# Inverse transform in pairs of 64-row tiles, spectra stored channel by channel, and a rewritten order

## The chip, the cores and the metric

One core of a Trainium2 chip runs the whole program. The time is that of one execution on the device in microseconds (us). The core has TensorE (PE; its weight loads are listed apart as PEld), VectorE (DVE), ScalarE (ACT), GpSimd (POOL) and SyncE (SP), and 16 DMA engines. Here all DMAs are issued by SP, in one queue.

## The reference

Two independent branches over 2048 positions and 576 channels in bfloat16, put side by side in the output.

```python
# A: a 4-tap causal filter over positions, times v; a long causal convolution by FFT; times q
k_shift = sum(k_pad[:, t:t + S, :] * shift_k[:, ks - 1 - t] for t in range(ks))
kv = k_shift * v
y_f = rfft(kv padded to 2S) * rfft(ssm_k padded to 2S)
y = irfft(y_f)[:S] + kv * ssm_D
a = q * y
# B: linear attention, 32 heads of 18 channels; phi(t) = (t + 1 if t > 0 else exp(t)) + 1e-6
pq, pk = phi(q), phi(k)                       # q, k, v = x @ wqkv
kv, z = einsum(pk, v), einsum(pk)             # sums over all positions
o = einsum(pq, kv) / (einsum(pq, z) + 1e-6)
b = o @ wo
```

## The kernel before

A kernel object (`Prog`) first collects about 800 operations with what each reads and writes. Then `PLAN`, a string written out by a planner beforehand, gives the order of all of them and the engine of each (`P` PE, `D` DVE, `A` ACT, `G` POOL, `S` SP), and `PLACES` gives the memory place of each buffer. An engine runs its own in this order. Products of two tensors ("two" operations) on DVE and POOL are made to follow one another.

Branch A. Position 16a + b lies on partition a, row b. The short filter (`conv_piece`, six pieces: three of 192 channels by two halves of b) is done by DVE with two products (`tap`, L374), one sum of 3072 columns, one of 1536, and a product with v (`tap+` and `tapv`, L229, by DVE or POOL); its second half needs the second load of k (`kh1`). The long convolution is an FFT in two steps. The filter `ssm_k` is loaded in six pieces of 96 channels (`hs`), transposed on PE (`htr`, L404) and evicted into `hT` (`hev`). `s1` multiplies by table G (L427, eight groups of four matmuls for each of three channel chunks; `s1h` for the filter, `s1u` for the signal, evicted to `Ch` and `Cu`). `s2` handles nine pieces of 64 channels: DVE transposes 32x32 blocks (`ct`, L447), PE does the 16-point step in 32-row array tiles (L457, four groups of four), and ACT or DVE evict the spectrum (`sph`, `spu`). `inv` exchanges real and imaginary rows by two DMAs (`X`) and makes the two products `p1` and `p2` (L229). The inverse 16-point step has two forms. For five pieces (`i1`, L515) a strided view of the products is the weight and a 128x128 block-diagonal table moves, so the result lands transposed in `V`:

```python
nc.tensor.matmul(o[:, 128 * c8:128 * c8 + 128],
                 lhsT=view(src.t[:], 4 * hh + c8, [[16, 128]]),
                 rhs=Esb.t[:, 32 + wi, :], start=(wi == 0), stop=(wi == 1))
```

For the four pieces in `TM` (`i1t`, L494) the table is the weight in 32-row tiles, the result is evicted to `yt`, and DVE transposes it into `V` (`tri`, L504). `inv2` does the last step with table E (L541, `i2`), for three groups of 192 channels; the result is evicted (`yb`, `yev`) and multiplied by q (`yq`), or multiplied by q straight from PSUM (`i2q`), and stored.

Branch B. x is loaded in four tiles and transposed (`xtr`, L315 and L313). `kproj` (L580) gives phi(k) through an exponential on ACT (L585) and one DVE instruction (`kphi`, L588); `qproj` (L601) does the same into `pqT` (ACT L604, DVE `qphi` L607). `b_G` (L630) sums x by pk over all positions; `kv` (L664), `den` (L700), a reciprocal and the folded output weight `M` (L720, L744) follow. The reciprocal goes through DRAM (`rw`, `rr`) to be spread, and five DVE products (`pqn`, L229) divide `pqT`. Each of the 32 groups of the output projection (`b_out`, L759, five matmuls) reads all five chunks of `pqT` and all of `M`; its result is evicted to `ob` (`oev`) and stored.

The helpers `copy` (L222 on ACT, L224 on DVE), `tt` (L229) and `dma` (L215) carry the evictions, products and DMAs of all steps, so those lines mix many groups.

Of the kernel before, what the change touches and what calls it, by code (L numbers as in the profile page):

```python
# [13 lines left out]
S = 2048  # L14
# [9 lines left out]
TM = [5, 6, 7, 8]  # L24
# [155 lines left out]
def kernel(  # L180
# [18 lines left out]
    G_d = nc.inline_tensor(Gt.reshape(128, -1), name="tab_g").ap()  # L199
# [75 lines left out]
    for i in range(2):  # L275
        load("Gsb", Gsb, lambda e, i=i: dma(e, Gsb.t[:, 8 * i:8 * i + 8].rearrange("p a b c -> p (a b c)"), G_d[:, 2048 * i:2048 * i + 2048]),
             524288, 4096, wr=[(Gsb, i)])
# [18 lines left out]

    def xt_load(g):
        load("x", x_sb, lambda e: dma(e, x_sb.t[:, 4 * g:4 * g + 4, :].rearrange("p a d -> p (a d)"),
                                      ap(x, 4 * g * D, [[16 * D, 128], [1, 4 * D]])),
# [4 lines left out]
        xTg.append(b)  # L304
        for t0, tn in ((0, 2), (2, 2), (4, 1)):
# [85 lines left out]
    hT = [SB("hT%d" % c, [128, 16, CC]) for c in range(3)]  # L391

    def h_piece(i):
        cc, hh = i // 2, i % 2
        hs = SB("hs", [96, S])
        load("hs", hs, lambda e: dma(e, hs.t[:], A_ssm_k[96 * i:96 * i + 96, :]), 393216, 4096, engs=EARLY)
        for half in range(2):
            ps = psb(1, "hps")

            def tr(e, half=half, ps=ps):  # L400
                o = ps.t.rearrange("p b c -> p (b c)").bitcast(BF)
                hv = hs.t[:].rearrange("d (a b) -> d b a", b=16)
                for j in range(8):
                    nc.tensor.transpose(out=o[:, 128 * j:128 * j + 96], in_=hv[:, 8 * half + j, :],  # L404
                                        identity=ident()[0:96, 0:96])

            def ev(e, half=half, ps=ps):
                i_ = ps.t.rearrange("p b c -> p (b c)").bitcast(BF).rearrange("p (j c) -> p j c", c=128)[:, :, 0:96]
                copy(e, hT[cc].t[:, 8 * half:8 * half + 8, 96 * hh:96 * hh + 96], i_)
            P.op("P", tr, rd=[hs, idw], wr=[ps], name="htr", mm=[(96, 96, 128)] * 8, st="htr%d" % i)  # L410
            P.op("DA", ev, rd=[ps], wr=[(hT[cc], (hh, half))], name="hev", n=768, x2=1, st="htr%d" % i)
        P.op("DG", lambda e: tt(e, hT[cc].t[0:1, 0, 96 * hh:96 * hh + 96], hT[cc].t[0:1, 0, 96 * hh:96 * hh + 96],
                                Drow.t[0:1, 96 * i:96 * i + 96], ALU.add),
             rd=[Drow], wr=[(hT[cc], (hh, 0))], name="hD", n=96, two=1, st="htr%d" % i)

    def s1(cc, nm):
        C = SB("C" + nm, [128, CC // 2, 32, 2])
        for ri in range(2):
            for bg in range(4):
                ps = psb(2, "s1ps")  # L420

                def mm(e, ri=ri, bg=bg, ps=ps):
                    for j in range(4):
                        b = 4 * bg + j
                        src = hT[cc].t[:, b, :] if nm == "h" else vs[bg // 2].t[:, b % 8, CC * cc:CC * cc + CC]
# [8 lines left out]
                rdk = [(vs[bg // 2], cc)] if nm == "u" else [hT[cc]]  # L434
# [7 lines left out]
    def s2(C, cc, pp, nm):  # L442
# [8 lines left out]
        sp = SB("sp" + nm, [128, 4, 512])  # L451
        for kh in range(4):
            ps = psb(1, "s2ps")

            def mm(e, kh=kh, ps=ps):
                for j in range(4):
                    nc.tensor.matmul(  # L457
                        ps.t[32 * j:32 * j + 32, 0, :].rearrange("p (k w t) -> p w k t", w=8, t=2),
# [3 lines left out]
            P.op("AD", lambda e, kh=kh, ps=ps: copy(e, sp.t[:, kh, :], ps.t[:, 0, :]),  # L462
# [10 lines left out]
    def inv(g, su):  # L473
# [5 lines left out]
        xb = SB("X", [128, 4, 512])  # L479
# [6 lines left out]
        if g in TM:  # L486
            yt = SB("yt", [128, 4, 512])
            for j in range(4):
                ps = psb(1, "i1ps")

                def mmt(e, j=j, ps=ps):
                    for kh in range(4):
                        for wi, src in ((0, tx), (1, xb)):
                            nc.tensor.matmul(  # L494
                                ps.t[32 * kh:32 * kh + 32, 0, :].rearrange("p (w k t) -> p k w t", w=8, t=2),
                                lhsT=Esb.t[32 * j:32 * j + 32, 32 + wi, 32 * j:32 * j + 32],
                                rhs=src.t[32 * j:32 * j + 32, kh, :], start=(wi == 0), stop=(wi == 1))
# [10 lines left out]
        for hh in range(4):  # L508
            ps = psb(1, "i1ps")

            def mm(e, hh=hh, ps=ps):
                o = ps.t.rearrange("p b c -> p (b c)")
                for c8 in range(4):
                    for wi, src in ((0, tx), (1, xb)):
                        nc.tensor.matmul(o[:, 128 * c8:128 * c8 + 128],  # L515
                                         lhsT=view(src.t[:], 4 * hh + c8, [[16, 128]]),
                                         rhs=Esb.t[:, 32 + wi, :], start=(wi == 0), stop=(wi == 1))
            P.op("P", mm, rd=[tx, xb, Esb], wr=[ps], name="i1", st=st, mm=[(128, 128, 128)] * 8)
# [4 lines left out]
            P.op("AD", ev, rd=[ps], wr=[(V[gi], (g, hh))], name="i1ev", n=512, st=st)  # L523
# [47 lines left out]
    def kproj(r):  # L571
# [5 lines left out]
        def mm(e):  # L577
            for hh in range(2):
                for t in range(5):
                    nc.tensor.matmul(ps.t[:, hh, 0:HALF],  # L580
                                     lhsT=xT.t[0:KT[t], t, 128 * (r % 4):128 * (r % 4) + 128],
# [169 lines left out]
    def b_out(r):  # L751
        ob = SB("ob", [128, D])
        for hh in range(2):
            ps = psb(1, "ops")

            def mm(e, hh=hh, ps=ps):
                for c, (h0, hn) in enumerate(HCH):
                    kn = 128 if c == 4 else hn
                    nc.tensor.matmul(ps.t[:, 0, 0:HALF], lhsT=pqT.t[0:kn, c, 128 * r:128 * r + 128],  # L759
# [5 lines left out]
        load("oo", None, lambda e: dma(e, ap(outd, 2 * D * r + D, [[32 * D, 128], [1, D]]), ob.t[:]), 147456, 1152, rd=[ob], wr=[])  # L765
# [4 lines left out]
    for cc in range(3):  # L770
        h_piece(2 * cc)
        h_piece(2 * cc + 1)
# [34 lines left out]
S27 S9 S7 P29 G0 A6 G2 P31 G3 S19 G4 G1 G55 P23 A28 D30 S12 D20 S352 P25 P21 A32 G14 S52 S51 P353 D22 S346 P355 A24  # L807
A26 P15 A16 D354 G357 D356 P33 P99 P93 S11 P347 S35 A100 D101 S57 P349 A94 D34 D348 G5 G351 D350 P96 G36 P370 D95
# [81 lines left out]
```

## Time and profile before

| | |
|---|---|
| runs (us) | 173.22, 173.25, 175.86; median 173.25 |
| the profiled execution: time, span | 173.95, 172.2 |
| busy us: PE, PEld, DVE, ACT, POOL | 159.2, 117.8, 144.8, 135.0, 66.2 |
| mean granted TensorE clock | 0.996 |
| DMA packets, MB, mean GB/s | 16327, 30.08, 175 |
| HBM read, written (MB) | 20.12, 4.98 |
| PE matmuls of the steps that change: L515, L494, L457, L404 | 160, 128, 288, 96 |

The span runs from the first to the last instruction of one execution; the time adds what lies around it. Busy time of an engine is the union of its instructions. A group in the profile reads: line, engine, operation, output <- inputs, shapes, count, then busy us and mean ns of one, then idle time just before it and what ended it. Instructions on one engine overlap a little, so count times mean can exceed the busy time.

### The profile page before, as it was taken

The page shows a single profiled execution, that of the slowest core. Times are in us where ns is not written, and L with a number is a line of the kernel's source. Part 1 is how long each engine was busy: PE and PEld are TensorE (multiplying, and loading weights), DVE is VectorE, ACT ScalarE, POOL GpSimd, SP SyncE. Part 2 cuts the span into 40 slices and gives each one's busy share as a digit, 9 for nine tenths or more (in the row PEclk, how much of TensorE's full clock was granted, in tenths as well). Part 3 has the DMA queues.
Part 4 walks back from the last instruction along what each step waited for, and adds up shares of the span by engine and source line. Part 5 has one row for each costly group of instructions (what it writes and reads, how often), then busy time and mean ns, then how long its engine had stood idle before and what let it go on. Part 6 is the DMA issues. An engine that isn't in the chain of part 4 may idle for free.

```text
span 172.2 us, 4216 instructions
## 1 busy us (share of the span) xinstructions
PE 159.2 (92%) x1718; PEld 117.8 (68%) x1718; DVE 144.8 (84%) x169; ACT 135.0 (78%) x239; POOL 66.2 (38%) x38
## 2 busy tenths in 40 slices
PE   0499999989999999999999999999999999998991
PEld 0386887736657766667666788759679766676880
DVE  0140799997999999999999999989979999989871
ACT  3334497969999999999999988899699999875200
POOL 7013100154009994291193001889560900473000
PEclk9999999999999999999999999999999999999998
DMA  5999999993000097800034339945148992176795
GB/s 161 267 235 322 245 287 238 271 265 86 7 2 0 0 292 244 313 11 0 0 126 166 130 67 308 296 149 197 61 131 272 253 354 124 41 214 174 233 272 175
DMA packets 16327, 30.08 MB, mean 175 GB/s; under 512 B 7571, under 2 KB 12308, under 8 KB 15540
## 3 DMA queue, kind: packets, MB, share of 16 engines
q1 hardware_dynamic: 16308, 29.82, 58.5%
q8 instruction: 13, 0.21, 0.5%
q14 instruction: 6, 0.05, 0.1%
HBM read 20.12 MB, written 4.98 MB: 146 GB/s over the span
## 4 chain that ended last, share of the span: by engine, by line
PE 44%; DMA 25%; DVE 19%; issue 6%; ACT 3%; SPq 1%; ACTq 0%; DVEq 0%
PE ps_all L630 12%; DMA wq<-in_B_wqkv_dram 10%; DMA kh<-in_A_k_dram 10%; PE ps_all L515 6%; DVE pqT L607 5%; PE ps_all L427 5%; PE ps_all L759 5%; DVE m L374 4%; PE ps_all L601 4%; DMA x_sb<-in_B_x_dram 4%; PE ps_all L457 4%; PE ps_all L541 3%; DVE pqT L229 2%; DVE m L229 2%; PE ps_all L664 1%
## 5 line engine op out<-in xcount | busy, mean ns | idle before, releaser
L601 PE MATMUL ps_all<-xT,wq 128*126 128x512 bf16 (+3 forms) x100 | 24.1, 381 | 0.4 <-DMA wq<-in_B_wqkv_dram 0.3
L580 PE MATMUL ps_all<-wk,xT 128*128 128x288 bf16 (+1 forms) x160 | 23.4, 299 | 0.3 <-DVE pk L588 0.3
L229 POOL TENSOR_TENSOR m<-m 128x1536 bf16<-128x1536 bf16 x5 | 15.5, 3103 | 16.8 <-ACT GT L641 7.2
L374 DVE TENSOR_TENSOR m<-kh,Wj 128x3072 bf16<-128x3072 bf16 x12 | 20.6, 1748 | 0.4 <-DMA kh<-in_A_k_dram 0.4
L759 PE MATMUL ps_all<-M,pqT 126*128 126x288 bf16 (+1 forms) x160 | 20.7, 285 | 0.2 <-DVE pqT L229 0.2
L222 ACT ACTIVATE Cu<-ps_all 128x768 bf16<-128x768 f32 x23 | 18.5, 865 | 1.6 <-PE ps_all L630 1.1
L580 PEld LDWEIGHTS <-xT 128*128 128x128 bf16 (+1 forms) x160 | 16.0, 102 | 5.3 <-issue 0.9
L222 ACT ACTIVATE sph<-ps_all 128x512 bf16<-128x512 f32 x33 | 19.0, 612 | 0.2 <-PE ps_all L457 0.2
L229 POOL TENSOR_TENSOR sph<-spu,sph 128x2048 bf16<-128x2048 bf16 x3 | 12.3, 4093 | 17.2 <-DVE X L229 15.2
L427 PEld LDWEIGHTS <-Gsb 128*128 128x128 bf16 x192 | 16.4, 98 | 3.6 <-issue 0.8
L759 PEld LDWEIGHTS <-pqT 126*128 126x128 bf16 (+1 forms) x160 | 15.3, 97 | 4.8 <-DVE pqT L229 0.5
L222 ACT ACTIVATE spu<-ps_all 128x512 bf16<-128x512 f32 x29 | 16.3, 609 | 2.0 <-PE ps_all L457 1.7
L601 PEld LDWEIGHTS <-wq 128*126 128x126 bf16 (+3 forms) x100 | 12.4, 131 | 7.7 <-issue 0.9
L222 ACT ACTIVATE ob<-ps_all 128x288 bf16<-128x288 f32 x21 | 7.9, 413 | 12.1 <-PE ps_all L759 11.5
L630 PE MATMUL ps_all<-pk,x_sb 128*128 128x288 bf16 (+1 forms) x128 | 17.1, 287 | 0.0
L222 ACT ACTIVATE Ch<-ps_all 128x768 bf16<-128x768 f32 x21 | 16.9, 848 | 0.2 <-PE ps_all L427 0.2
L588 DVE SCALAR_TENSOR_TENSOR pk<-ek,ps_all 128x576 bf16<-128x576 bf16 x16 | 11.8, 739 | 5.5 <-ACT ek L585 5.5
L585 ACT ACTIVATE ek<-ps_all,neg 128x576 bf16<-128x576 f32 x16 | 12.0, 750 | 4.8 <-PE ps_all L580 3.1
L229 POOL TENSOR_TENSOR hT<-hT,Drow 1x96 bf16<-1x96 bf16 x5 | 3.7, 746 | 30.2 <-DVE hT L224 12.9
L630 PEld LDWEIGHTS <-x_sb 128*128 128x128 bf16 x128 | 12.1, 97 | 4.2 <-issue 1.3
L604 ACT ACTIVATE eq<-ps_all,neg 126x512 bf16<-126x512 f32 (+1 forms) x20 | 13.4, 712 | 0.5 <-PE ps_all L601 0.3
L457 PE MATMUL ps_all<-ct,idw 32*32 32x512 bf16 x288 | 13.8, 382 | 0.0
(97 smaller groups left out, 347.8 us busy)
## 6 DMA issues: line engine op xcount, KB each, us to landing
X<-sph SPq DMA_DIRECT2D x18, 256.0 KB, 2.8
x_sb<-in_B_x_dram SPq DMA_DIRECT2D x4, 576.0 KB, 3.9
hs<-in_A_ssm_k_dram SPq DMA_DIRECT2D x6, 384.0 KB, 10.3
v<-in_A_v_dram SPq DMA_DIRECT2D x2, 1152.0 KB
q<-in_A_q_dram SPq DMA_DIRECT2D x1, 2304.0 KB
out_dram<-ob SPq DMA_DIRECT2D x16, 144.0 KB, 2.0
out_dram<-q SPq DMA_DIRECT2D x12, 192.0 KB, 2.5
rb<-r_scr SPq DMA_DIRECT2D x4, 504.0 KB
```

The lines of the kernel that those rows point to most:

```text
L222: nc.scalar.activation(out=o, in_=i, func=ACTF.Copy)
L229: return (nc.vector if e == "DVE" else nc.gpsimd).tensor_tensor(out=o, in0=a, in1=b, op=op)
L374: return nc.vector.tensor_tensor(out=m.t[:, i:i + 2], in0=i0, in1=i1, op=ALU.mult)
L427: nc.tensor.matmul(ps.t[:, bank, lo - 384 * bank:hi - 384 * bank], lhsT=Gsb.t[:, b, ri, :], rhs=src[:, lo - CC * j:hi - CC * j], start=Tru ...
L457: nc.tensor.matmul(ps.t[32 * j:32 * j + 32, 0, :].rearrange("p (k w t) -> p w k t", w=8, t=2), lhsT=W2()[32 * kh:32 * kh + 32, :], rhs=ct. ...
L580: nc.tensor.matmul(ps.t[:, hh, 0:HALF], lhsT=xT.t[0:KT[t], t, 128 * (r % 4):128 * (r % 4) + 128], rhs=wk.t[0:KT[t], t, HALF * hh:HALF * hh ...
L585: P.op("A", lambda e: nc.scalar.activation(out=eb.t[:], in_=ps.t[:, :, 0:HALF], func=ACTF.Exp, bias=neg1.t[:]), rd=[ps, neg1], wr=[eb], na ...
L588: P.op("D", lambda e: nc.vector.scalar_tensor_tensor(out=pk.t[:, r, 0:D].rearrange("p (h c) -> p h c", h=2), in0=eb.t[:], scalar=1.0, in1= ...
L601: nc.tensor.matmul(ps.t[0:hn, 0, :], lhsT=wq.t[0:KT[t], t, h0:h0 + hn], rhs=xT.t[0:KT[t], t, :], start=(t == 0), stop=(t == 4))
L604: P.op("A", lambda e: nc.scalar.activation(out=eb.t[0:hn], in_=ps.t[0:hn, 0, :], func=ACTF.Exp, bias=neg1.t[0:hn, :]), rd=[ps, neg1], wr=[eb],
L630: nc.tensor.matmul(ps.t[0:m, 0, 0:n], lhsT=x4.t[:, r, 0:65] if t == 4 else x_sb.t[:, r, 128 * t:128 * t + 128], rhs=pk.t[:, r, HALF * hh:H ...
L759: nc.tensor.matmul(ps.t[:, 0, 0:HALF], lhsT=pqT.t[0:kn, c, 128 * r:128 * r + 128], rhs=M.t[0:kn, c, HALF * hh:HALF * hh + HALF], start=(c ...
```

## The change

1. `s2` writes its PSUM bank with the channel outermost, and the spectra `sph`, `spu` and `X` become [128, 16, 128] (channel, then position index) where they were [128, 4, 512].
2. `TM` becomes empty: all nine pieces take the form `i1`. A piece is done in two halves into two PSUM banks. Each 128-row matmul becomes two of 64 rows, one for each half of the array's rows (z), with the 64 columns of its own block of the table, each into its own bank, with a column step of eight. One eviction of 1024 columns follows each half.
3. The filter comes in pieces of 128 channels (four of 128, one of 64) into one `hT` of 576 channels.
4. The table G lies in DRAM with rows of 2304 values, of which 2048 are read.
5. A tile of x holds 512 consecutive positions, four on each partition; the stores of branch B follow that order. A second way to load x (`XD`) is written but its list is empty.
6. `PLAN` and `PLACES` are new: 774 operations for 820. On PE all eight `s1h` groups of the first chunk stand ahead of the first `kproj`; on SP three tiles of x, two filter pieces and both halves of G stand ahead of most of wk; the 32 output groups stand at the very end.

```diff
-TM = [5, 6, 7, 8]
+TM = []
+XD = []
...
-    G_d = nc.inline_tensor(Gt.reshape(128, -1), name="tab_g").ap()
+    Gp = np.zeros((2, 128, 2304), Gt.dtype)
+    Gp[:, :, 0:2048] = Gt.reshape(128, 2, 2048).transpose(1, 0, 2)
+    G_d = nc.inline_tensor(Gp.reshape(256, 2304), name="tab_g").ap()
...
+    def cols(t, r):
+        if r // 4 in XD:
+            return view(t, r % 4, [[4, 128]])
+        return t[:, 128 * (r % 4):128 * (r % 4) + 128]
...
-                                      ap(x, 4 * g * D, [[16 * D, 128], [1, 4 * D]])),
+                                      ap(x, 512 * g * D, [[4 * D, 128], [1, 4 * D]])),
...
-    hT = [SB("hT%d" % c, [128, 16, CC]) for c in range(3)]
+    hT = SB("hT", [128, 16, D])
     def h_piece(i):
-        cc, hh = i // 2, i % 2
-        hs = SB("hs", [96, S])
+        h0, hn = 128 * i, min(128, D - 128 * i)
+        hs = SB("hs", [hn, S])
...
-        sp = SB("sp" + nm, [128, 4, 512])
+        sp = SB("sp" + nm, [128, 16, 128])
...
-                        ps.t[32 * j:32 * j + 32, 0, :].rearrange("p (k w t) -> p w k t", w=8, t=2),
+                        ps.t[32 * j:32 * j + 32, 0, :].rearrange("p (w t k) -> p w k t", w=8, t=2),
                         lhsT=W2()[32 * kh:32 * kh + 32, :], rhs=ct.t[32 * kh:32 * kh + 32, 8 * j:8 * j + 8],
...
-            P.op("AD", lambda e, kh=kh, ps=ps: copy(e, sp.t[:, kh, :], ps.t[:, 0, :]),
+            P.op("AD", lambda e, kh=kh, ps=ps: copy(
+                e, sp.t[:, :, 32 * kh:32 * kh + 32], ps.t[:, 0, :].rearrange("p (c k) -> p c k", c=16)),
...
-        for hh in range(4):
-            ps = psb(1, "i1ps")
+        for hh in range(2):
+            ps = psb(2, "i1ps")
             def mm(e, hh=hh, ps=ps):
-                for c8 in range(4):
+                for c in range(8):
                     for wi, src in ((0, tx), (1, xb)):
-                        nc.tensor.matmul(o[:, 128 * c8:128 * c8 + 128],
-                                         lhsT=view(src.t[:], 4 * hh + c8, [[16, 128]]),
-                                         rhs=Esb.t[:, 32 + wi, :], start=(wi == 0), stop=(wi == 1))
+                        for z in range(2):
+                            nc.tensor.matmul(view(ps.t, 512 * z + c, [[8, 64]]),
+                                             lhsT=src.t[64 * z:64 * z + 64, 8 * hh + c, :],
+                                             rhs=Esb.t[64 * z:64 * z + 64, 32 + wi, 64 * z:64 * z + 64],
+                                             start=(wi == 0), stop=(wi == 1))
...
-                copy(e, view(V[gi].t[:], c0 + 4 * hh, [[n, 32], [16, 4], [1, 4]]),
-                     ps.t.rearrange("p b c -> p (b c)").rearrange("p (c j r) -> p r j c", j=4, r=32))
+                copy(e, view(V[gi].t[:], c0 + 8 * hh, [[16, 4], [n, 32], [1, 8]]),
+                     ps.t.rearrange("p b (j r c) -> p (b j) r c", r=32, c=8))
...
-        load("oo", None, lambda e: dma(e, ap(outd, 2 * D * r + D, [[32 * D, 128], [1, D]]), ob.t[:]), 147456, 1152, rd=[ob], wr=[])
+        load("oo", None, lambda e: dma(e, ap(outd, 2 * D * (512 * (r // 4) + r % 4) + D, [[8 * D, 128], [1, D]]), ob.t[:]), 147456, 1152, rd=[ob], wr=[])
...
-        h_piece(2 * cc)
-        h_piece(2 * cc + 1)
+        for i in ((0, 1), (2,), (3, 4))[cc]:
+            h_piece(i)
```

More of the change, by code (lines that the diff above doesn't have):

```diff
@@ L403, in tr @@
                 for j in range(8):
[L404 to L405 removed]
+                    nc.tensor.transpose(out=o[:, 128 * j:128 * j + hn], in_=hv[:, 8 * half + j, :],
+                                        identity=ident()[0:hn, 0:hn])
             def ev(e, half=half, ps=ps):
[L408 to L414, printed above, removed]
+                i_ = ps.t.rearrange("p b c -> p (b c)").bitcast(BF).rearrange("p (j c) -> p j c", c=128)[:, :, 0:hn]
+                copy(e, hT.t[:, 8 * half:8 * half + 8, h0:h0 + hn], i_)
+            P.op("P", tr, rd=[hs, idw], wr=[ps], name="htr", mm=[(hn, hn, 128)] * 8, st="htr%d" % i)
+            P.op("DA", ev, rd=[ps], wr=[(hT, (i, half))], name="hev", n=8 * hn, x2=1, st="htr%d" % i)
+        P.op("DG", lambda e: tt(e, hT.t[0:1, 0, h0:h0 + hn], hT.t[0:1, 0, h0:h0 + hn], Drow.t[0:1, h0:h0 + hn], ALU.add),
+             rd=[Drow], wr=[(hT, (i, 0))], name="hD", n=hn, two=1, st="htr%d" % i)
     def s1(cc, nm):
```

98 lines of the change are left out of this document (51 added, 47 removed), and 29 rows, old and new, of the table PLACES.

## The prediction

> **What bounds the kernel now.** I read the busy shares first, then the engines by stage, then who waits in the long stage, then the single rows around the change.
>
> ```profile
> PE 159.2 (92%) x1718; PEld 117.8 (68%) x1718; DVE 144.8 (84%) x169; ACT 135.0 (78%) x239; POOL 66.2 (38%) x38
> ```
>
> PE looks like the bound. The busy time by stretches, cut at the start of the first short-filter product on DVE (31.06) and at the end of the last division product (143.62), corrects that. The columns are start:end, length, then busy time and instructions of each engine, granted clock, DMA share and GB/s.
>
> ```profile
> 0.00:31.06 31.06, 23.98 (x238) 19.84 (x239) 14.98 (x24) 16.51 (x23) 6.57 (x16) 1.00 0.97 254
> 31.06:143.62 112.56, 110.98 (x1230) 79.24 (x1227) 108.36 (x116) 105.23 (x186) 53.10 (x18) 1.00 0.49 154
> 143.62:172.20 28.58, 24.26 (x253) 18.73 (x253) 21.43 (x32) 13.29 (x33) 6.54 (x4) 0.97 0.58 169
> ```
>
> In the middle 112.56 us PE is busy 110.98, DVE 108.36 and ACT 105.23: three engines are full at once, so taking work from one alone gains nothing there. The first stretch is a load stage (DMA share 0.97), the last is the output projection. The waits of DVE inside the middle stretch, the longest first, are tiny:
>
> ```profile
> DVE M L224 <- POOL sph L229: 0.9, 1, 0.9
> DVE pqT L607 <- ACT eq L604: 0.5, 1, 0.5
> ```
>
> Two rows of DVE's order in time mark the hinges: the first filter product, and the division products (pqn), without which no output projection can start, because every one reads all five chunks of pqT.
>
> ```profile
> 31.06 1.74 DVE L374 TENSOR_TENSOR m<-kh,Wj 128x3072 bf16<-128x3072 bf16 x1
> ...
> 138.99 4.63 DVE L229 TENSOR_TENSOR pqT<-pqT,rb 126x2048 bf16<-126x2048 bf16 x4
> ```
>
> So the span of 172.2 is 31.06 (to the first product) + 112.5 (DVE's row up to the last pqn) + 28.6 (what is left). I forecast each of the three.
>
> The rows of the changed steps, groups with shapes kept apart:
>
> ```profile
> L457 PE MATMUL ps_all<-ct,idw 32*32 32x512 bf16 x288 | 13.8, 382 | 0.0
> L515 PE MATMUL ps_all<-Esb,sph 128*128 128x128 bf16 x80 | 11.4, 228 | 0.3 <-ACT spu L222 0.3
> L515 PE MATMUL ps_all<-Esb,X 128*128 128x128 bf16 x80 | 11.3, 227 | 0.0
> L494 PE MATMUL ps_all<-sph,Esb 32*32 32x512 bf16 x64 | 3.5, 381 | 0.1
> L504 DVE STREAM_TRANSPOSE V<-yt 128x1024 f32<-128x1024 f32 x4 | 7.7, 1957 | 0.8 <-ACT yt L222 0.8
> L222 ACT ACTIVATE V<-ps_all 128x512 bf16<-128x512 f32 x15 | 8.5, 624 | 0.0
> ```
>
> Instructions overlap their neighbours, so I price by the distance between starts when an engine runs back to back: on DVE the row's mean less 0.08 us (four pqn in 4.63: 1.14 each, mean 1.217), on ACT the mean less 0.13 (512 columns: 0.48, not 0.61). On PE eight L515 matmuls start 62 ns apart, 128x128 transposes 56, 512 columns 216.
>
> **The change, part by part.** *Inverse 16-point step on PE.* Before: five pieces of 32 matmuls (20 groups, 10.9 us from start to next start) and four pieces in 32-row tiles (16 groups, 4.3 us). After: nine pieces of 64 matmuls of 64 rows by 64 columns, in 18 halves of 32, each alternating between two row tiles and two banks. No row shows such a tile. Lower end: both row tiles run at once, 16 rounds of 64 columns; 512 take 216 ns and 128 take 56, so 64 take 29, a half 0.47. Upper end: each weight load follows the other at L515's 62 ns, a half 2.0. The nearest row is L457: 24 of its small tiles, with 24 loads, take 0.62 us (110.66 on), 26 ns a pair against 216 for one alone, so row tiles and their loads do run together. I take 0.5: 9.0 us, and 1.9 for the eight places at which PE enters this tile size (a 64-row matmul among 128-row ones stretches two intervals from 58 to 150 and 195 ns in L664: 0.23). The 32-row runs fall from 29 to 21 without the four pieces: 17.1 us to some 10.3 (0.33 alone, 0.68 for six). Together PE's inverse and 16-point steps go from 28.1 to 21.2.
>
> [...]
>
> *The same step elsewhere.* DVE loses four transposes (1.83 to 1.88 each, 7.4) and seven evictions (0.59, 4.1). ACT has 18 evictions of 1024 columns for 29 of 512: 1024 is 0.92 (between 0.48 for 512 and 1.03 for Wj's 1152), so 16.5 for 13.9: +2.6.
>
> *Spectra channel by channel.* Same matmuls, copies and X transfers, other strides. Matmul writes now go 32 words apart where pairs were adjacent; ends: 0, or half speed, 0.22 more in some 30 rounds, 6.5 us on PE. L457 already writes with gaps at full speed: 0.
>
> *Filter pieces of 128.* 96 transposes become 80 at 62 ns: PE -1.0. Six loads become five with the same bytes; twelve evictions of 768 become ten, eight of them of 1024: DVE gets seven of 0.61 for five of 0.48 (+1.8), ACT three for seven (-2.9).
>
> *Padded table rows, x in blocks of four consecutive rows.* Bytes and instructions stay. 1.05 MB at 245 GB/s is 4.3 us, at the best slice's 322 it is 3.3: a gain of 0 to 1.0 ahead of the forward step; none shows for x or for the output rows, which follow x. I take 0, behind loads that are queued anyway.
>
> *New plan.* This decides. **First stretch:** SP now queues three x tiles, two filter pieces and both halves of the table G before most of wk; G's end is 3.98 MB down the queue (4.70 before). At the slices' 161 to 322 GB/s 4.0 MB are in by 16.5, and x0 landed 2.4 later than this count says (8.67 in the chain): 19. PE then does all eight s1h groups (L427) before any k projection. Transposes do not bring it to full speed (16 took 1.87 us at 4.86 and 1.07 at 33.73; the first 20 of L580 took 4.21, later 20 2.63), so these eight take 4 us, not 2.6. Six k groups of 1.24, one htr and one s1h follow: 31.5; exp and min/max of k4 (0.65 each) stand ahead of the first product: 32.4, against 31.06. kh, now 7.0 MB down the queue instead of 6.7, lands by 30 and is no bound.
>
> **Middle:** DVE's row from the first product to the last pqn. Out: six i1 evictions 3.5, one V transpose 1.8, one ct transpose now earlier 1.2, two GT 0.9, one v product 0.9, one spectrum eviction 0.6, gcol 0.2. In: four products p1, p2 (L229, 1.14 each) 4.6, four yb evictions 1.9, xT 1.2, s1 0.9, a tap sum 0.9, filter 0.8, M 0.7, i2q 0.5, hD 0.1. That is 107.1 before, 109.5 after; DVE's gaps were 5.4 and I keep them. kh's second half waits on another buffer now (kh0, free after the sixth product) and lands 6.9 later with 6.3 of DVE work ahead of it, a wait of 0.6 where 0.4 was. On SP the load of q (2.4 MB) now stands ahead of the reciprocal's way out and back: free after G at some 112, 10 us at 245 GB/s, done before the reciprocal is (125); the way back (3.6 and another 10) is in by 139, ahead of the first pqn at 141. POOL's products fall from 66 to 64 us and stay beside DVE's. The last pqn ends at 32.4 + 109.5 + 5.4 = 147.3, 3.7 later than before. ACT agrees: 101.4 of work from there to the last V eviction (100.0 before in the same 112.4) ends at 145.4, and the plan puts one i2 product, which needs V, ahead of the last pqn. From k4's end PE has 107 left (21.2 as above, 85.7 of other groups at their distances), ends them by 139 and waits some 8 us: that is where its saving goes, and it is the cover for the upper ends above.
>
> **Last stretch:** before, PE had eight i1t, eight i2 groups and 32 projection groups left and DVE 20.7 us. After, 32 x 0.617 + 2 x 0.33 = 20.4 on PE against 12.2 on DVE; the last matmul's end lay 3.8 before the span's. 24.2, against 28.6.
>
> **Sum:** 147.3 + 24.2 = 171.5, 0.7 below 172.2. The profiled execution took 173.95, inside the 173.22 to 175.86 of the runs shown but 0.7 above their median; on the median of 173.25 the sum gives **172.5**.
>
> **Rivals.** *The saving shows whole.* DVE's total falls by 4.4 (142.1 to 137.7 by these prices), ACT's by 3.9, PE's by 7. If the kernel is paced by totals, not by this order, 173.25 - 4.4 = 168.9. For it: three full engines all lose work. Against: DVE's saving lies behind the last pqn, where PE sets the end. Chance 0.20.
>
> [...] Chance 0.08.
>
> *The forward step ahead of k starves DVE.* If G lands as late as 22.5, the first product goes to 36 and the end to 176.1; slower than now from 33.1 on. For it: 19 rests on one lag, and nothing else feeds DVE then. Against: 2 MB of slack in front of kh. Chance 0.17 for over 1 us slower, about half of it over 2%.
>
> *The new strides halve PSUM writes.* 6.5 on PE, under the cover of 8: 172.5 to 174, inside the forecast's range. Chance 0.05.
>
> **How the numbers follow.** Forecast, within 2% of now (2% is 3.5 us, about what a measurement of this kernel can tell from no change): chance 0.50, own range 170 to 175. With the first rival up to 169.8, 0.20; from the second and third above 176.7, 0.07 and 0.09. Faster by over 2%: 0.20; slower by over 2%: 0.16; within: 0.64. The range 168.5 to 177.0 holds the first rival whole and the third but for its tail, and leaves out most of the serial loads.
>
> **What would show it.** Right: a first L374 near 32.4, the last pqT product near 147, 32 L759 groups in one unbroken run behind it, PE waiting some 8 us in the middle (for DVE and ACT), a half of the inverse step near 0.5 us. Wrong: i1 matmuls 62 ns apart (serial loads); the first L374 past 34; or a last pqT product ahead of 144, which would mean that DVE's order was not the bound.

## The result and the profile after

The changed kernel takes 180.09 us (median of 179.22, 180.09, 180.71 and 180.09) against 173.81 for the kernel before: a ratio of 1.037 with an interval of 1.030 to 1.044. It is slower, by some 6 us; the forecast was 172.5. The kernel before was run again beside each of the five sets of experiments below, at medians of 173.16, 173.76, 173.70, 173.50 and 172.76, so a difference of 1 us between runs of different sets says little. Times given are medians over all executions, with the lowest and highest in brackets; the ratios to the kernel before, with 95% intervals in square brackets, leave out executions that were disturbed.

The profiled execution has a span of 177.4. First its busy times, then the chain that ended last (its first line, by engine):

```profile
PE 164.9 (93%) x1990; PEld 119.8 (68%) x1990; DVE 140.7 (79%) x172; ACT 131.6 (74%) x214; POOL 61.6 (35%) x35
...
PE 86%; DMA 5%; SPq 3%; DVE 2%; issue 1%; ACT 1%; DVEq 0%
```

DVE, ACT and POOL did lose work, 4.1, 3.4 and 4.6 us. PE, which was to lose 7, gained 5.7, and the chain is PE's for 86% of the span. The stretches, cut as before at the first short-filter product (29.72) and the end of the last division product (153.24); columns as in the prediction:

```profile
0.00:29.72 29.72, 22.61 (x229) 19.09 (x230) 16.43 (x25) 17.41 (x24) 5.42 (x13) 1.00 0.95 300
29.72:153.24 123.52, 121.86 (x1598) 84.68 (x1596) 110.56 (x119) 108.89 (x177) 49.69 (x18) 1.00 0.38 133
153.24:177.40 24.16, 20.44 (x167) 16.02 (x167) 13.68 (x30) 5.31 (x14) 6.47 (x4) 1.00 0.66 196
```

The first stretch is 1.3 shorter than before and the last 4.4, but the middle is 11.0 longer. In it PE is busy for all but 1.7 us, while DVE, busy 110.6 of 123.5, now waits. Its longest waits there:

```profile
DVE spu L227 <- ACT GT L657: 2.6, 1, 2.6
DVE kvb L683 <- ACT V L225: 2.6, 1, 2.6
DVE q L232 <- ACT yb L225: 2.3, 1, 2.3
DVE yb L227 <- PE ps_all L557: 2.0, 1, 2.0
```

Before, the two longest were 0.9 and 0.5. Each of these was ended by a PE group or by the eviction of one. The two steps of PE that the change touched, and the one place where PE stood still in the middle (second fence, PE's waits):

```profile
L471 PE MATMUL ps_all<-ct,idw 32*32 32x512 bf16 x288 | 19.0, 605 | 0.0
L530 PE MATMUL ps_all<-Esb,X 64*128 64x64 bf16 x288 | 17.3, 243 | 1.6 <-issue 1.6
L530 PE MATMUL ps_all<-Esb,sph 64*128 64x64 bf16 x288 | 17.2, 242 | 0.0
```

```profile
PE ps_all L530 <- issue: 1.6, 1, 1.6
```

The 16-point step L471 (L457 before) does the same 288 matmuls at 605 instead of 382 ns. From start to next start its groups take 17.6 us (12.7 before) and the 18 halves of L530 18.7, a half 0.88 when the next one follows at once. Together 36.3, where the two steps had 28.1 before, by the prediction's count, and 21.2 in the forecast. "issue" means that PE waited for nothing that the profile shows: a wait of an unknown kind inside L530.

### The profile page after: what moved, and what is told of

The parts are those of the page before. It is cut to its first block, busy times and chain, and to the rows that moved or that the text cites. A ratio compares the mean times of both kernels' runs of the same rounds, so it can differ in the third digit from the quotient of the medians.

```text
span 177.4 us, 4739 instructions
## 1 busy us (share of the span) xinstructions
PE 164.9 (93%) x1990; PEld 119.8 (68%) x1990; DVE 140.7 (79%) x172; ACT 131.6 (74%) x214; POOL 61.6 (35%) x35
## 4 chain that ended last, share of the span: by engine, by line
PE 86%; DMA 5%; SPq 3%; DVE 2%; issue 1%; ACT 1%; DVEq 0%
PE ps_all L617 13%; PE ps_all L646 11%; PE ps_all L596 11%; PE ps_all L775 11%; PE ps_all L471 10%; PE ps_all L530 10%; PE ps_all L441 9%; DMA Gsb<-tab_g 5%; PE ps_all L557 4%; SPq L218 3%; PE ps_all L419 2%; PE ps_all L680 2%; PE ps_all L736 1%; PE ps_all L760 1%; DVE hT L227 1%
## 5 line engine op out<-in xcount | busy, mean ns | idle before, releaser
L225 ACT ACTIVATE V<-ps_all 128x1024 bf16<-128x1024 f32 x18 | 17.6, 1032 | 5.8 <-PE ps_all L530 5.8
L232 POOL TENSOR_TENSOR X<-spu,X 128x2048 bf16<-128x2048 bf16 x3 | 12.2, 4066 | 24.2 <-ACT Cu L225 16.3
L471 PE MATMUL ps_all<-ct,idw 32*32 32x512 bf16 x288 | 19.0, 605 | 0.0
L530 PE MATMUL ps_all<-Esb,X 64*128 64x64 bf16 x288 | 17.3, 243 | 1.6 <-issue 1.6
L232 POOL TENSOR_TENSOR v<-m,v 128x1536 bf16<-128x1536 bf16 x5 | 15.5, 3095 | 8.6 <-DVE m L232 5.5
L232 POOL TENSOR_TENSOR m<-m 128x1536 bf16<-128x1536 bf16 x4 | 12.4, 3098 | 16.4 <-DVE m L232 10.9
L225 ACT ACTIVATE Cu<-ps_all 128x768 bf16<-128x768 f32 x22 | 17.6, 854 | 0.5 <-PE ps_all L441 0.5
L225 ACT ACTIVATE ob<-ps_all 128x288 bf16<-128x288 f32 x14 | 5.3, 410 | 16.1 <-PE ps_all L775 15.6
L530 PE MATMUL ps_all<-Esb,sph 64*128 64x64 bf16 x288 | 17.2, 242 | 0.0
L530 PEld LDWEIGHTS <-X 64*128 64x128 bf16 x288 | 16.1, 120 | 1.7 <-issue 1.7
L646 PE MATMUL ps_all<-pk,x_sb 128*128 128x289 bf16 (+1 forms) x128 | 17.1, 287 | 0.0
L225 ACT ACTIVATE spu<-ps_all 128x512 bf16<-128x512 f32 x29 | 15.5, 605 | 1.8 <-PE ps_all L471 1.6
```

The source lines that it names most:

```text
L225: nc.scalar.activation(out=o, in_=i, func=ACTF.Copy)
L232: return (nc.vector if e == "DVE" else nc.gpsimd).tensor_tensor(out=o, in0=a, in1=b, op=op)
L471: nc.tensor.matmul(ps.t[32 * j:32 * j + 32, 0, :].rearrange("p (w t k) -> p w k t", w=8, t=2), lhsT=W2()[32 * kh:32 * kh + 32, :], rhs=ct. ...
L530: nc.tensor.matmul(view(ps.t, 512 * z + c, [[8, 64]]), lhsT=src.t[64 * z:64 * z + 64, 8 * hh + c, :], rhs=Esb.t[64 * z:64 * z + 64, 32 + w ...
L646: nc.tensor.matmul(ps.t[0:m, 0, 0:n], lhsT=x4.t[:, r, 0:65] if t == 4 else x_sb.t[:, r, 128 * t:128 * t + 128], rhs=pk.t[:, r, HALF * hh:H ...
```

## Experiments

Theory A: matmuls that write PSUM words which are not neighbours run at about half rate, in both steps. The rivals: the 64-row tiles or their loads set the pace, or the new order of the plan does.

**The 16-point step, either side put in order.** s2_pairs writes neighbouring pairs again and lets the eviction sort the columns:

```diff
-ps.t[...].rearrange("p (w t k) -> p w k t", w=8, t=2)     # matmul out
+ps.t[...].rearrange("p (k w t) -> p w k t", w=8, t=2)
-ps.t[:, 0, :].rearrange("p (c k) -> p c k", c=16)         # eviction in
+ps.t[:, 0, :].rearrange("p (k c) -> p c k", c=16)
```

> The changed kernel with one part undone: the 16-point step (L471) again writes its PSUM bank in the old order (neighbouring pairs, then 16 words on), and the eviction puts the columns into the new order. Theory A, that words written 32 apart one after the other run at about half rate, expects L471 back from 605 to about 380 ns a matmul, a single group from 0.54 to 0.33 us start to next, some 5 us less on PE, and as PE is the bound up to the last pqn, 175 us (174 to 176.5). Rival B, that the 16-point step is slower because of what surrounds it in the new order (waits for evictions, no write cost), expects 605 ns and 180 us as before the edit. Rival C, that the eviction pays for the order instead, expects PE relieved but the ACT rows of these evictions longer and 178 us or more.

s2_read writes the new order in neighbouring words and reads the moving operand out of order instead:

```diff
-ps.t[...].rearrange("p (w t k) -> p w k t", ...), rhs=ct.t[...]
+ps.t[...].rearrange("p (w t k) -> p w t k", ...), rhs=ct.t[...].rearrange("p w k t -> p w t k")
```

> The changed kernel with the 16-point step's write in neighbouring words, in the new column order, and its moving operand read out of order instead (single elements 4 bytes apart). Theory A (the write order alone costs) expects L471 at about 380 ns a matmul, five us less on PE than the changed kernel, 175 us. Rival B (either side of the step, out of order, halves it) expects 600 ns still and 180 us.

Measured 174.85 (174.36 to 176.11) and 175.16 (173.90 to 176.24). The step's row in each, s2_pairs first:

```profile
L471 PE MATMUL ps_all<-ct,idw 32*32 32x512 bf16 x288 | 12.0, 383 | 0.3 <-DVE Cu L227 0.2
```

```profile
L471 PE MATMUL ps_all<-ct,idw 32*32 32x512 bf16 x288 | 12.3, 391 | 0.2 <-DVE Cu L227 0.2
```

Both are back at the 382 ns of the kernel before or close to it (11.0 and 11.2 us from start to next start, for 17.6) and 5 us faster than the changed kernel. A moving operand read 4 bytes apart costs almost nothing here (391 ns against 383), nor does an eviction that reads PSUM 16 words apart (ACT's evictions into `sph` have a mean of 623 ns in s2_pairs and 617 in s2_read, which reads them in order); only the side that the matmul writes counts. A holds for this step, and the new order of the plan is not what slows it.

**The same write in the kernel before.** before_s2 puts the new write order into the old kernel and lets the eviction sort the columns back (`sp.t[:, kh, :].rearrange("p (k c) -> p c k", c=16)` as its output); before_s2_bare leaves the eviction alone.

> The kernel before with one part of the change alone: the 16-point step writes its PSUM bank in the new order, words 32 apart, and its eviction puts the columns back, so that all that follows is as before. Theory A expects L457 at 605 in place of 382 ns a matmul, 17.6 in place of 12.8 us on PE from start to next; PE is busy without a pause over most of the stretch where these stand, but waits some 8 us near its end, so 2 to 5 us of it show: 175 to 178.5 us. Rival B (the slow step comes from the order of the new plan) expects 382 ns and 173.2 us.

> The kernel before with the 16-point step's write order alone: words 32 apart in PSUM, and the eviction copies the bank straight through as before, so what follows works on spectra whose columns are permuted; nothing else of the computation is touched and no eviction is. In the run in which the eviction put the columns back, ACT's 128x512 evictions took 2530 ns (they stored single elements 32 bytes apart) and hid all else. Theory A: L457 at 605 in place of 382 ns, 4.8 us more on PE from start to next, of which 2 to 5 us show: 175 to 178.5 us. Rival B (the slow step comes from the new order of the plan): 382 ns and 173.5 us.

before_s2 took 285.16 us, far outside every expectation, for a reason of its own: its evictions, which now stored single bf16 elements 32 bytes apart.

```profile
L222 ACT ACTIVATE sph<-ps_all 128x512 bf16<-128x512 f32 x33 | 77.7, 2530 | 1.4 <-PE ps_all L457 1.4
L222 ACT ACTIVATE spu<-ps_all 128x512 bf16<-128x512 f32 x29 | 68.2, 2612 | 6.2 <-PE ps_all L494 4.3 <-PE ps_all L457 1.9
```

The same evictions stored straight through take 600 ns in before_s2_bare. That run came out at 179.08 us (178.32 to 181.74), a ratio of 1.031 [1.025, 1.037], with the matmul row of the changed kernel:

```profile
L457 PE MATMUL ps_all<-ct,idw 32*32 32x512 bf16 x288 | 21.1, 603 | 0.0
```

So the write order alone makes the old kernel 5.4 us slower. Most of the 6.7 us of added PE time (19.4 from start to next, from 12.7) shows. The "some 8 us" of waiting that the expectation counted on are not there: in the kernel before PE idles 1.6 us of the whole middle stretch (110.98 busy of 112.56, in the prediction's fence), and 6.7 less 1.6 is 5.1.

**The 64-row pairs, written in runs, or undone.** i1_runs writes each pair's 64 columns as neighbours; i1_128 goes back to one matmul over all 128 rows, also in runs:

```diff
-nc.tensor.matmul(view(ps.t, 512 * z + c, [[8, 64]]), lhsT=src.t[64 * z:64 * z + 64, ...], ...
+nc.tensor.matmul(ps.t[:, z, 64 * c:64 * c + 64], lhsT=src.t[64 * z:64 * z + 64, ...], ...     # i1_runs
+nc.tensor.matmul(o[:, 128 * c:128 * c + 128], lhsT=src.t[:, 8 * hh + c, :], rhs=Esb.t[:, 32 + wi, :], ...  # i1_128
```

> The changed kernel with the inverse's 64-row pairs (L530) writing 64 neighbouring words each instead of 64 words 8 apart; the eviction reads the columns in the order it needs. Theory A (two row tiles run side by side, and the write 8 words apart holds each at half rate) expects a half of 32 matmuls at 0.45 to 0.5 us in place of 0.88, some 7 us less on PE, 173 to 174 us. Rival B (the two row tiles do not run side by side, or the 64-column loads of their weights set the pace at 27 ns a matmul, whatever the write order) expects 0.88 us still and 180 us.

> The changed kernel with the 64-row pairs undone alone: 16 matmuls a half over all 128 rows with the 128-column block table, neighbouring words, weights loaded from 128 neighbouring columns; the 16-point step as in the changed kernel. Theory A: 16 x 54 ns or a little more, 0.88 to 0.96 us a half, so the pairs as they stand are worth nothing here: 179.5 to 181 us. Rival B expects the same 0.88. A half well under 0.8 would say that the pairs themselves cost time; one over 1.05 that they save some.

i1_runs: 178.82 us (177.53 to 180.03); i1_128: 177.06 (176.38 to 178.81). In i1_runs the halves that followed one another freely took 0.467 to 0.49 us: 14.6 ns a matmul, load included. So the two row tiles do run side by side, and the write step had doubled their time. i1_128 takes 0.893 a half, 56 ns a matmul. The kernel with pairs as changed was thus no faster on PE than whole-array matmuls. But where is i1_runs' gain? Its halves sum to 13.4 us for 18.7, waits included, and the time fell by 1.3 only:

```profile
L530 PE MATMUL ps_all<-Esb,sph 64*128 64x64 bf16 x288 | 10.9, 196 | 0.4 <-DVE M L763 0.3 <-ACT spu L225 0.2
L530 PE MATMUL ps_all<-Esb,X 64*128 64x64 bf16 x288 | 10.8, 195 | 2.4 <-issue 2.4
```

The unexplained wait has grown to 2.4; a second one of 1.6 follows in L680, and behind that the granted clock was 0.50 from 130.6 to 137.4, where two halves took 0.88 and 1.02. s2_pairs and s2_read have such a wait too, of 1.9 and 2.2 us in L530; i1_128 has none.

**Both in order; and both rows without taking turns.** both_runs joins s2_pairs and i1_runs. i1_runs_noalt is i1_runs with the loop over z outermost, so that all 16 matmuls of rows 0 to 63 come first.

> Both edits: the 16-point step writes in the old order and the 64-row pairs write neighbouring words. Theory A: 11 to 12 us less on PE than in the changed kernel, more than DVE's own row leaves room for (first filter product at 29.7, DVE's work of 109.5 and gaps of 5.4 up to the last pqn at about 144.6, then 24.2, and 2.7 around the span): 171.5 us (170 to 173). Rival B: only the 16-point step gains, 175 us. If the new order itself costs the time, 178 us or more.

> The run with 64-row pairs in neighbouring words, with the two halves of the array no longer taken in turn: all 16 matmuls of rows 0 to 63 first, then all 16 of rows 64 to 127. Theory A (two row tiles overlap, and only when they alternate) expects a half at 16 x 2 x 27 = 0.87 us in place of 0.47, and with so slow a use of instructions a shorter pause (1.5 instead of 3 us): 178.5 to 180.5 us. The rival (a 64-row matmul of 64 columns costs 14.5 ns by itself, without any overlap) expects 0.47 us still, and 178.8 us.

both_runs: 173.54 us (173.06 to 175.81), 2 above the expectation. i1_runs_noalt: 183.90 (181.51 to 185.72), slower than either side expected: its free halves take 0.735 to 0.785, neither 0.87 nor 0.47, so alternating rows is worth a factor of 1.6; it has a wait of 2.3 us, and its granted clock was 0.50 from 128.1 to 141.8. In both_runs the stretches from 118 to 126 (columns as above):

```profile
118.00:120.00 2.00, 1.08 (x61) 0.87 (x54) 2.00 (x1) 2.00 (x4) 1.94 (x2) 1.00 1.01 423
120.00:122.00 2.00, 0.00 (x0) 0.00 (x0) 2.00 (x2) 1.57 (x2) 0.39 (x1) 0.91 0.54 221
122.00:124.00 2.00, 1.99 (x76) 1.99 (x77) 2.00 (x3) 0.97 (x2) 0.00 (x0) 0.50 0.29 84
124.00:126.00 2.00, 1.66 (x62) 1.47 (x56) 1.49 (x2) 1.54 (x3) 0.38 (x1) 0.73 0.38 119
```

PE starts nothing for 3.1 us in the middle of a half, a wait that the profile calls only "issue", and then has a granted clock of 0.50. The DMA traffic from 114.3 to 119.4 (first line below: packets, MB, share) has no packet on the instruction queue (q8), and that from 119.4 to 120.6 has one, of 16,384 bytes:

```profile
q1 hardware_dynamic: 283, 2.07, 106.5%
```

```profile
q1 hardware_dynamic: 26, 0.48, 96.2%
q8 instruction: 1, 0.02, 5.6%
```

A half of 0.47 us has 64 loads and matmuls. The q8 packets go with PE's instructions: 13 of them in the runs with 3,404 or 3,436 loads and matmuls, 14 with 3,692, 15 with 3,980, so one for some 260.

**Is it the supply of instructions?** pairs_128 joins s2_pairs and i1_128 (half the instructions); i1_128_split is i1_128 with each matmul cut into two of 64 columns (twice as many).

> The 16-point step written in neighbouring pairs and the inverse as 128-row matmuls, 16 a half: half as many instructions on PE in the inverse as with 64-row pairs. In the run with both steps in runs PE stood still for 3.1 us in the inverse, for which the profile shows no other engine to wait for, and an instruction block of 16 KB arrived in that time; after it the granted clock was 0.50 for some 8 us. Theory I (256 instructions of one block are used up faster than the next is brought when a half of 64 loads and matmuls takes 0.47 us) expects no such pause, 0.89 us a half, a clock of 1.00 throughout, and 171 to 173 us, no more than with the pairs although its matmuls take 7 us longer. The rival (the pause is a wait for an X load or a PSUM bank) expects the pause to stay and 175 us or more.

> The run with 128-row matmuls in the inverse (16-point step as in the changed kernel), each matmul cut into two of 64 columns: the same PE time by the columns (32 x 27 ns, 0.87 us a half), twice as many instructions, as many as the pairs have. Theory I expects a pause of 1 to 3 us in the inverse as in the changed kernel, 1.5 to 3 us more than the uncut 128-row matmuls (177.06 us): 178.5 to 180.5 us. The rival (instructions don't matter; the row tiles, or what they wait for, do) expects 177 us and no pause.

pairs_128: 171.88 us (171.39 to 172.50), no pause, clock 1.00; ratio to the kernel before 0.988 [0.983, 0.993]. i1_128_split: 179.84 (179.46 to 180.57), 2.8 more than i1_128, or 2.2 when each is taken from the kernel before beside it. Its free halves take 0.93 for 0.89, and it has two waits of "issue" where the uncut kernel has none:

```profile
PE ps_all L530 <- issue: 2.5, 2, 1.6
```

Both runs came out as theory I said. The stretches of pairs_128:

```profile
0.00:30.33 30.33, 22.42 (x229) 19.00 (x230) 16.39 (x25) 17.23 (x24) 5.43 (x13) 1.00 0.94 304
30.33:145.10 114.77, 114.19 (x1310) 85.00 (x1308) 109.57 (x118) 107.14 (x178) 49.75 (x18) 1.00 0.41 141
145.10:169.60 24.50, 20.71 (x170) 16.01 (x167) 14.01 (x31) 5.42 (x14) 6.47 (x4) 1.00 0.66 193
```

**Why the block comes late.** mixed takes whole-array matmuls for each piece's first half and pairs in runs for the second. The four runs named "qlate" move one DMA of the plan, the load of q, behind the store of the row sums:

```diff
-... P660 S92 P690 ...
-... G700 S241 P706 ...
+... P660 P690 ...
+... G700 S241 S92 P706 ...
```

> The 16-point step written in neighbouring pairs, the inverse's first halves (columns 0 to 7 of each piece's sixteen) as 128-row matmuls and its second halves as 64-row pairs into neighbouring words: 18 halves of 0.89 and 0.47 us, 48 instructions a half on average. Theory I says that a block of 256 instructions comes at best every 3.5 us (13.7 ns an instruction); eight halves in a row use 384 in 5.4 us, 14 ns each, so no pause over 1 us, and 3.8 us less on PE than with 128-row matmuls throughout (171.88 us). DVE's row then sets the end: 171 us (170 to 172). If the pause hangs on the pairs themselves it comes back: 173 us or more.

> The run with both steps in neighbouring words (64-row pairs), and the load of q (2.36 MB, issued at 112 us, with the DMA engines at a share of 1.0 until 119.5) issued behind the store of the row sums instead, at about 121; its first use is at about 131. The 16 KB instruction block came at 119.5, just as that load ended, in three runs with different numbers of instructions used by then. Theory Q (the block waits behind q's packets) expects a block at 115 to 118, no pause over 1 us before 123, a clock of 1.00 throughout there, and 170 to 171.5 us in place of 173.54. Rival I alone (256 instructions used faster than a block can come, whatever else the DMA engines do) expects the pause of 3 us to stay, and 173.5 us.

> The run with 128-row matmuls for the first halves and 64-row pairs for the second, with q's load issued at 121 us. There the pause stayed at 2.8 us against my expectation. Theory Q expects no pause and 169.5 to 171 us, 2 to 3 us less than with q early (173.08); rival I alone 173 us.

> The run with neighbouring pairs and 128-row matmuls throughout, which had no pause (171.88 us), with q's load issued at 121 us: what the move does by itself. Both theories expect 171.5 to 172 us, and the rows of the row sums' way back or of q's first products to show it if the late load hinders them (up to 174).

> The changed kernel as it is, but q's load issued behind the store of the row sums. Its pause is 1.6 us with 64 instructions a half of 0.88 us. Theory Q: the pause goes, 178.3 us (177.5 to 179.2) in place of 180.1. Rival I alone: 180 us.

mixed missed: 173.08 (170.11 to 174.11), with a wait of 1.8 us in its profile again (not 2.8, as the expectation of mixed_qlate has it). Its stretch from 120 to 122, and the same of mixed_qlate:

```profile
120.00:122.00 2.00, 0.22 (x3) 0.22 (x4) 2.00 (x3) 2.00 (x3) 0.58 (x1) 0.96 0.67 278
```

```profile
120.00:122.00 2.00, 2.00 (x82) 1.79 (x75) 2.00 (x2) 2.00 (x4) 1.30 (x2) 1.00 0.04 8
```

With q out of the way the instruction block comes sooner after the one before it: 3.4 to 3.6 us for 6.2 to 6.7, in each of five pairs of runs (the changed kernel, both_runs, mixed, pairs_128 and the pair of flat runs below). The pause at this place is gone wherever there was one. So theory Q, a block held up while q's load runs, holds for this pause; by what means the load holds it up is not shown.

What that is worth in time is less clear. after_qlate takes 178.53 (178.32 to 179.37), 1.6 less than the changed kernel, but its ratio to the kernel before is 1.035 [1.026, 1.044] for 1.037, and a new wait of 0.9 us stands in it around 142. mixed_qlate takes 171.35 (170.01 to 173.65), 1.7 less than mixed. Yet mixed's five shortest executions of twelve (170.1 to 172.1) lie among those of mixed_qlate, and the two ratios, 0.989 [0.984, 0.994] and 0.991 [0.987, 0.995], don't differ. mixed_qlate too has a new wait, 1.7 us around 139. pairs_128_qlate took 171.41 (170.30 to 171.82), the move alone being worth 0.5 at most.

both_runs_qlate stayed at 173.61 (172.87 to 176.37), against the expectation. Its profile shows two things that can have taken the place of the pause; neither was tested alone. Its halves run into ACT: four in a row take 0.92 each, with ACT's evictions of 1024 columns in one unbroken row,

```profile
118.16 5.63 ACT L225 ACTIVATE V<-ps_all 128x1024 bf16<-128x1024 f32 x6
```

0.94 each. There a half of 0.47 on PE is worth nothing. And the clock falls to 0.50 from about 124 to 131, and a second pause (1.7 us, in the half at 136.5) comes while the DMA engines are busy again (share 0.92 from 134 to 136). The number of instructions matters all the same: pairs_128 has no pause although its q load lies where it did, and no two blocks came closer together than 3.3 us in any of these runs.

The traces hold stronger evidence that PE waits for instructions. Count PE's loads and matmuls in the order in which they start. The pause stands behind the 2487th in the changed kernel, s2_pairs, s2_read, i1_runs, i1_runs_noalt, both_runs and i1_128_split, and behind the 2486th in mixed, though another matmul stands there in mixed. The other pauses of more than 0.7 us (from start to start) that end on no other engine stand behind the 2232nd, 2742nd, 3253rd (mixed_qlate: 3252nd) and 3508th. These places lie 255 or 511 apart, to within one, which is about one packet's worth or two (theory I counted with 256), and each such pause ends 1.3 to 1.5 us after a q8 packet has landed. A wait for an X load or a PSUM bank would not keep to such a count.

**What remains.** pairs_128_flat has the table G unpadded, pairs_128_flat_qlate that and the late q; i1_128_apart4 is pairs_128 with the inverse's 128 columns written 4 words apart.

> The run with neighbouring pairs and 128-row matmuls (171.88 us), with the table G laid out as before the change: rows of 8192 bytes, each half of a row loaded for itself, no padding. Theory: the padding shortens the load (it landed at 14.66 us in the changed kernel and about 18 before) and with it the first filter product; undone, the first stretch is 1 to 1.5 us longer, 173 us (172 to 174). The rival (the load hides behind the x transposes): 171.9 us.

> Neighbouring pairs in the 16-point step, 128-row matmuls in the inverse, the table G unpadded and q's load behind the store of the row sums: the edits together that cost nothing or gained. Each by itself moved the time by 0.5 to 1 us at most from 171.88, so 170.5 us (170 to 171.5) is expected; 171.9 if they do not add.

> The run with neighbouring pairs in the 16-point step and 128-row matmuls in the inverse (171.88 us), the inverse's 128 columns now written 4 words apart, four columns of the spectra interleaved in a bank. If any step apart costs (theory A in general, whole rows and whole array too), a matmul takes about 107 in place of 56 ns and a half 1.7 in place of 0.89 us: 18 x 0.8 = 15 us more on PE, 185 us (182 to 188). If only far steps cost (8 and 32 words were seen), 0.89 us a half and 172 us. If what costs is the 64-row tile written apart, 172 us as well.

Unpadded: 170.91 (170.39 to 172.00), 0.986 [0.982, 0.990] of the kernel before; the padding is worth nothing. With q late as well: 171.55 (170.38 to 172.82), 0.994 [0.990, 0.998]. pairs_128, with and without either edit, lies between 170.9 and 171.9; three of the four intervals are below 1 (that of pairs_128_qlate reaches 1.0005), and I don't rank them. They beat the changed kernel, and the one before by about 1% (by 0.5% and not clear of noise in pairs_128_qlate). i1_128_apart4, run once, took 186.33 us, as A expected for any distance and whole-array matmuls too:

```profile
L529 PE MATMUL ps_all<-Esb,X 128*128 128x128 bf16 x144 | 32.2, 314 | 0.0
L529 PE MATMUL ps_all<-Esb,sph 128*128 128x128 bf16 x144 | 31.9, 312 | 0.3 <-ACT V L225 0.2
```

With neighbouring words (pairs_128) the two rows have 219 ns; from start to next a half goes from 0.89 to 1.75 us, 109 ns a matmul for 56.

## Why the prediction was wrong

**The step that failed** is "L457 already writes with gaps at full speed: 0". L457 wrote pairs of neighbours and then left a gap; single words 32 apart are another thing. The term was 0. The step measured 17.6 us on PE for the 10.3 forecast, 7.3 more: 6.6 of it is the write order (17.6 against 11.0 in s2_pairs), the other 0.7 the size of the runs. I had the term's size as the upper end (6.5) and chose the wrong end, by the nearest-looking row. The runs show that single words apart slow the matmul, and by how much: 109 for 56 ns a matmul with steps of 4 words, 0.88 for 0.467 us a half with steps of 8, 0.54 for 0.33 us a lone group with steps of 32. Not every gap does so: neighbouring pairs with gaps between them cost no more than unbroken runs (383 ns in s2_pairs, 391 in s2_read). Why single words are slow isn't shown, and no step of 2 words was run.

**The same omission in the inverse step.** Here I weighed tiles and loads but not the column step of eight in the same line of code. Forecast 9.0 + 1.9, measured 18.7, of which the pause is 1.6. The lower end of 0.47 a half was exact, once the words were neighbours (0.467); a half at the start or end of a run of them takes 0.10 to 0.17 more where nothing else holds it, for the 0.23 forecast. The pause, 1.6 us, was in no term and no rival.

Loads that follow one another, the upper end of 2.0 a half (chance 0.08), were the wrong mechanism: in i1_runs a load and its matmul take 14.6 ns from start to start. A single load is far longer, by the loads' own rows of i1_runs:

```profile
L530 PEld LDWEIGHTS <-sph 64*128 64x128 bf16 x288 | 9.8, 98 | 1.9 <-issue 1.8
L530 PEld LDWEIGHTS <-X 64*128 64x128 bf16 x288 | 9.8, 99 | 2.5 <-issue 2.5
```

But 288 loads of 98 ns fit into 9.8 us, so they run beside one another and beside the matmuls. L457, which I took as the nearest row, was no fair witness on this: its loads have 32 columns (88 ns each in the kernel before), not 128. And a half needed far less than 2.0 to cost time. The cover of 8 over 18 halves, added to the 0.5 taken, gives 0.94; without the pause the mean was 0.95, and the 16-point step's 7.3 came on top.

**One cover spent twice.** Each upper end was held against the same 8 us of PE's waiting. The two steps came out 15.1 us over the forecast together (36.3 for 21.2). PE's list, forecast to end by 139, would end by 139 + 15.1 - 2.7 (the earlier start) = 151.4; it ran with no gap but the pause, which the 15.1 include, up to the first projection group at 152.90. The last 1.5 us stay open. DVE's work in the middle is as forecast: busy 110.6, for 108.4 before and 2.4 to be added; but it waits 13.0 there, where before it waited 4.2. So the bound moved from DVE's order to PE, and the rival "The new strides halve PSUM writes" was right about the step (605 ns a matmul for 382), with a price (up to 174) that leaned on a cover already gone. before_s2_bare shows how little cover there was even before: 5.4 of 6.7 us came through. Its chance of 0.05 was far too low.

**What held.** The last stretch: 24.2 forecast, 24.2 measured. ACT's 1024 columns: 0.92 forecast, 0.94 measured. With the write steps and the pause taken away (pairs_128), the sum comes near: last pqn 145.1 for 147.3, 24.5 for 24.2, span 169.6 for 171.5, time 171.88 for 172.5. That is partly luck. PE was to save 7 us and wait some 8 in the middle; in pairs_128 its two steps take 11.0 and 16.3 us, 27.3 for the 28.1 before, and it is busy 114.19 of 114.77. DVE waits 5.2 there, as forecast, but PE is just as full, so the run doesn't show that DVE's order sets the end.

**First stretch.** "19" for G's landing rested on x0's lag; G was used from 15.5 and the first product came at 29.72, not 32.4. The 4 us for the eight s1h groups rested on transposes that don't bring PE to full speed, and the changed kernel shows otherwise: its transposes started 107 ns apart from 8.17 and 56 ns apart from 11.8, and the s1h matmuls behind them 82 ns apart from the first (16.26) on, 3.31 us for all 32 with three short gaps. The padding that I also considered has no part in it: in pairs_128_flat, without it, the first product comes at 29.04, for 30.33 in pairs_128.

**Where the 6.3 us come from.** Undoing the step in the 16-point write gives 5.2, undoing the pairs with their step and their pause 3.0, both together 8.2 (180.09 to 171.88), so they add, within the 1 us by which sets differ; the rest of the change, which these runs don't split further except for the padding, gains 1.9 (173.81 to 171.88).

## What to carry to other kernels

Look at the order in which a matmul's columns fall into PSUM: in these runs neighbours (391 ns) and neighbouring pairs (383) cost the same, single words apart took 1.6 to 2 times as long from start to next (17.6 for 11.0 us in the 16-point step, 109 for 56 ns a matmul in the inverse), and the reordering belongs on the read side, the moving operand's or the eviction's. Hold the upper ends of all unknown costs on one engine against its idle time together, not one by one. When many small matmuls replace few, count the instructions and ask what the DMA engines carry at that moment, and whether the eviction can follow.

## What the runs showed of the hardware

- Matmul writes to PSUM: 0.33 us for a lone 16-point group in pairs or in runs and 0.54 with words 32 apart; 56 against 109 ns for 128 columns 4 words apart; 0.467 against 0.88 us for a half of pairs 8 apart.
- Two 64-row tiles taken in turn, in neighbouring words: 14.6 ns a matmul of 64 columns, its load included (i1_runs); the same without turns 23 ns (i1_runs_noalt).
- The queue that the profile calls instruction (q8) brought packets of 16,384 bytes, 13 to 15 in a run, one for some 260 of PE's loads and matmuls. They came 3.3 us apart at best, and 6.2 to 6.7 while the 2.36 MB load of q ran. PE stood still, at places 255 or 511 loads and matmuls apart, until 1.3 to 1.5 us after a packet had landed; its waits say only "issue".
- The granted clock fell to 0.50, for 3.4 to 13.7 us, after waits of 1.8 (mixed), 2.3 (i1_runs_noalt), 2.4 (i1_runs) and 2.9 us (both_runs), but not after 1.9 (s2_pairs), 2.2 (s2_read) or the changed kernel's 1.6. In both_runs_qlate it fell though PE was busy 2.6 of the 4 us before. What decides it was not tested.
- An ACT eviction of 128x512 that stores bf16 elements 32 bytes apart takes 2530 ns (before_s2) instead of 600 (before_s2_bare).
